# Attention over packed keys and two expert layers on one core: how W' is stored, which engine issues the word loads, and the order of the packed attention's steps

## The chip, the cores and the metric

The kernel runs on one core of one Trainium2 chip. The metric is device microseconds of one execution. The times given are medians of several runs; the profile is of one execution, and its span runs from the first to the last instruction.

## The reference

Inputs are q, k, v of 8 batches x 8 heads x 576 tokens x 64 and p of 8 x 8 x 32 x 64, all float32, and four float64 weight matrices. With 4608 tokens of width 512:

```
def sm_attn(qq, kk, vv):
    s = scale * np.matmul(qq, kk.transpose(0, 1, 3, 2))
    a = np.exp(s - np.max(s, axis=-1, keepdims=True))
    a = a / (np.sum(a, axis=-1, keepdims=True) + 1e-09)
    return np.matmul(a, vv)
p_packed = sm_attn(p, k, v)
out = sm_attn(q, p_packed, p_packed)
x = (tokens x 512 view of out)
h = x @ w_in;  g = h * np.cos(h);  x2 = g @ w_out          (first layer, w_in 512 x 2048)
h = x2 @ w_in2;  P = a0 + a1 h + a2 h^2 + a3 h^3
Q = 1 + |b0| |h| + |b1| h^2;  out = (P / (Q + 1e-6)) @ w_out2   (second layer)
```

## The kernel before, in words

Three stages follow each other, with some overlap.

The **packed attention** works on 16 groups (a batch and four of its heads). For group n the helper `prep` transposes k into kT on DVE (L180), `s1` makes the scores of p against k on PE (L189), their maximum (mx, L203) and scaled negative (nb, L205) on DVE, and the exponentials E on ScalarE (L208); `et` transposes E on PE (L224) and copies it to eT on ScalarE (L226); `pv` multiplies it with v on PE (L235), scales and masks the result into ppm on DVE (L239) and stores it to ppd; `ppt` transposes ppm on PE (L258) and splits it into the high and low part wl (L66 ScalarE, L67 DVE). pbd is p transposed into blocks, at the start, on DVE (L168). The second attention of batch 0 is woven in between (`attn2_steps`).

The **W' stage** multiplies wl with w_in, so that h later comes straight from the attention weights. There are 16 units (4 column blocks fq x 4 head pairs hp), and in each unit 4 tiles (P, a pair of batches) of 128x512 on PE (L275). A tile is evicted from the accumulator by ScalarE (L286), the third of each unit by DVE (L284), into one of four wev buffers, and stored to the scratch tensors wd. `load_wq` brings the parts of wd that a batch needs back as wq, and `split_wq` divides them into high and low part. Four of the first layer's slots (below) run early, in between.

The weights are float64 and are read as pairs of 32-bit words. A load brings 128x1024 words (512 KB) into one of three st64 buffers; `convert` makes a float32 pair from them: ScalarE scales the low word (L80), DVE does three integer steps on the high word (L82, L87, L90), GpSimd multiplies (L91, the last reader of st64), DVE adds (L92), ScalarE rounds to the high part (L93), GpSimd subtracts for the low part (L94). `conv_next` emits one conversion and the load three conversions ahead.

The **rest** is PE's: 128 slots of the first layer (h L520, y L567) and then the second layer (L671, L729).

The program is written in one order, and a scheduler then decides for each engine in which order its instructions stand; an engine's queue runs strictly in that order. The DMA queues are SP's (k, v, q, words, wq) and ScalarE's (ppd, W' stores).

Of the kernel before, what the change touches and what calls it, by code (L numbers as in the profile page):

```python
# [20 lines left out]
def pack_attention_moe_moe_kernel(  # L21
# [78 lines left out]
    NP = B // 2  # L100
    wd = [dram.tile([B, G, 128, 512], F32, name=f"wd{i}") for i in range(NQ)]
    ppd = [dram.tile([128, 4 * D], F32, name=f"ppd{n}") for n in range(NG)]
# [10 lines left out]
    if True:  # L113
# [19 lines left out]
        def load_v(n):  # L133
            b, g = divmod(n, G)
            t = wv.tile([96, 4, 6 * D], F32, tag="vx", bufs=3, name="vx")
            nc.sync.dma_start(out=t, in_=v[b, 4 * g:4 * g + 4].rearrange("h (x r) d -> x h (r d)", r=6))
            vx_t[n] = t
# [22 lines left out]
        for h in range(4):  # L160
            nc.gpsimd.memset(mask[32 * h:32 * h + 32, h, :], 1.0)
        load_kv(1)

        pbd = wv.tile([128, NG, NDB, 4, M], F32, name="pbd")
# [10 lines left out]
        def prep(n):  # L175
            b, g = divmod(n, G)
            kT = wk.tile([128, NDB, 6, 32, 3], F32, tag="kT", bufs=2, name="kT")
            kx = kx_t.pop(n)
            for e in range(NDB):
                nc.vector.transpose(  # L180
                    out=kT[:, e].rearrange("p r j a -> p a r j"),
                    in_=kx[:, :, 32 * e:32 * e + 32].rearrange("p (a r) i -> p a r i", a=3),
                )
            kT_t[n] = kT.rearrange("p e r j a -> p e (r j a)")

# [79 lines left out]
        def wunit(x):  # L265
            fq, hp = cv1[x]
            wi = w1i_t.pop(x)
            g, gg = divmod(hp, 2)
            dst = wd[fq].rearrange("(c b) g p f -> c b g p f", b=2)
            for P in range(NP):  # L270
                t = we_p.tile([128, 512], F32, tag="wev", bufs=4, name="wev")
                ps = psw.tile([128, 512], F32, tag="w", bufs=2, name="w")
                wl = wl_t[P]
                for i, (a, c) in enumerate(PASSES):
                    nc.tensor.matmul(  # L275
                        out=ps,
                        lhsT=wl[a][:, hp].rearrange("p b m -> p (b m)"),
                        rhs=wi[c],
                        start=(i == 0),
                        stop=(i == 2),  # L280
                    )

                if P == 2:
                    nc.vector.tensor_scalar(out=t, in0=ps, scalar1=INV2PI, scalar2=None, op0=ALU.mult)  # L284
                else:
                    nc.scalar.activation(out=t, in_=ps, func=AF.Copy, scale=INV2PI)  # L286
                for b2 in range(2):
                    nc.scalar.dma_start(out=dst[P, b2, g, 64 * gg:64 * gg + 64], in_=t[64 * b2:64 * b2 + 64])  # L288

# [62 lines left out]

        def load_st(x, src):
            t = cv_p.tile([128, 512, 2], U32, tag="st64", bufs=3, name="st64")
            if len(src.shape) == 4:
                ld = nc.sync.dma_start(out=t.rearrange("p (k f) t -> p k f t", k=NKD), in_=src)
            else:
                ld = nc.sync.dma_start(out=t, in_=src)
            st_t[x] = t
            return ld  # L360
# [5 lines left out]
        def load_w1i(x):  # L366
            fq, hp = cv1[x]
            load_st(("i", x), words(w1i[128 * hp:128 * hp + 128, 512 * fq:512 * fq + 512]))

# [6 lines left out]
        def load_w1o(f):  # L376
            load_st(f, words(w1o[128 * f:128 * f + 128, :]))

# [27 lines left out]
        for i in range(3):  # L406
# [4 lines left out]
            0, wk, lambda nm: ps0.tile([128, 2, 512], F32, tag="s1", bufs=2, name=nm), tg0, lambda: None  # L411
        )
        for n in range(NG + 1):
            if n >= 3:
                next(at, 1)
            if n < NG:
                s1(n)
                if n + 2 < NG:
                    load_kv(n + 2)
            if n >= 1:  # L420
                pv(n - 1)
            if n + 1 < NG:
                prep(n + 1)
            if n < NG:
                et(n)
            if n % 3 and at_cv[0] < NA:
                conv_next()
            if n >= 1:
                ppt(n - 1)
# [12 lines left out]
        def load_wq(b, j):  # L442
            t = wo_p.tile([128, G, 2, 512], F32R, tag="wq", bufs=5, name="wq")
            nc.sync.dma_start(
                out=t[:, :, 1, :].bitcast(F32),
                in_=wd[j][b].rearrange("g p f -> p g f"),
            )
            wq_t[b, j] = t
# [5 lines left out]
        def load_w2(i):  # L454
# [3 lines left out]
            else:  # L458
                src = words(w2o[128 * f:128 * f + 128, :])
            hold(load_st(("w2", i), src), last_h[0])  # L460

# [167 lines left out]
        for x in range(len(cv1)):  # L629
# [4 lines left out]
            if x in more:  # L634
                conv_next()
            if hp == NKD - 1:
                load_wq(0, fq)
            if fq > 0 and hp == 2:
                split_wq(0, fq - 1, nc.vector)
            if x in early:  # L640
                slot(early.index(x))
        e0.close()
        at_p = e1t.enter_context(tc.tile_pool(name="at", bufs=1, side="right", **RW))
# [147 lines left out]
```

## Time and profile before

| | us |
|---|---|
| median of 3 runs (lowest, highest) | 1713.13 (1712.69, 1714.67) |
| the profiled execution's own time | 1714.48 |
| its span | 1712.7 |
| PE busy | 1616.1 (94%) |
| DVE busy | 1325.6 (77%) |
| ScalarE (ACT) busy | 1197.7 (70%) |
| GpSimd (POOL) busy | 184.8 (11%) |
| mean granted TensorE clock | 0.981 of full speed |

A share of the span is an average over stages with different limits, and PE's matmuls are pipelined with modelled ends. Issuing a DMA is not counted as busy: a queue can be full while its engine looks idle. "ACTq" and "SPq" are the queues of ScalarE and SP.

### The profile page before, as it was taken

What the parts mean: (1) busy time and instruction counts of PE and PEld (TensorE: products, weight loads), DVE (VectorE), ACT (ScalarE), POOL (GpSimd) and SP (SyncE); (2) the same over time, 40 slices, a digit from 0 to 9 for tenths busy, and PEclk for the clock granted to TensorE, in tenths of its full rate; (3) what the DMA queues carried; (4) which work ended last, traced back from release to release, by engine and by line L of the source; (5) the groups of instructions that cost most, each with busy time, mean ns of one, the idle gap of its engine ahead of it and who ended that gap; (6) DMA issues with size and microseconds to landing.
All of it is one profiled execution on the core that took longest, in us unless ns stands there. A gap on an engine that the chain in (4) does not pass through costs nothing.

```text
span 1712.7 us, 23880 instructions
## 1 busy us (share of the span) xinstructions
PE 1616.1 (94%) x8832; PEld 1408.8 (82%) x8832; DVE 1325.6 (77%) x2054; ACT 1197.7 (70%) x1933; POOL 184.8 (11%) x140
## 2 busy tenths in 40 slices
PE   6786768999999999999999999999999999999996
PEld 4674658999999999999998888888888888888884
DVE  8954665879787888878548888888888888888884
ACT  3434645767676777767659787778777878787874
POOL 4303540012121211121000000000000000000000
PEclk9998888999999999999999999999999999999998
DMA  9857773434343443434276101101020202020100
GB/s 303 264 162 197 225 206 102 133 125 154 131 156 120 143 153 122 144 131 151 90 259 214 50 25 37 38 24 51 1 74 1 74 1 74 1 74 1 41 10 25
DMA packets 104372, 183.49 MB, mean 107 GB/s; under 512 B 12096, under 2 KB 46912, under 8 KB 104256
## 3 DMA queue, kind: packets, MB, share of 16 engines
q1 hardware_dynamic: 91712, 163.09, 29.4%
q10 hardware_dynamic: 12544, 18.88, 4.2%
q8 instruction: 69, 1.13, 0.3%
q14 instruction: 47, 0.39, 0.1%
HBM read 117.97 MB, written 63.96 MB: 106 GB/s over the span
## 4 chain that ended last, share of the span: by engine, by line
PE 79%; DVE 4%; ACT 3%; issue 1%; DMA 1%; ACTq 1%; POOL 1%; DVEq 0%; POOLq 0%; SPq 0%
PE h L671 23%; PE o L729 23%; PE y L567 20%; PE h L520 11%; PE s L189 2%; ACTq L288 1%; DVE g L552 1%; ACT u L545 1%; PE w L275 0%; POOL cvp L91 0%; DVE cvf L87 0%; ACT r L550 0%; ACT r L551 0%; DVE sT L340 0%; DVE cvf L82 0%
## 5 line engine op out<-in xcount | busy, mean ns | idle before, releaser
L567 PE MATMUL y<-gh,w1o 128*128 128x288 f32 x2048 | 432.7, 297 | 0.4
L671 PE MATMUL h<-x,w 128*128 128x512 f32 x1728 | 422.2, 393 | 0.0
L671 PEld LDWEIGHTS h<-x,w 128*128 128x128 f32 x1728 | 324.1, 188 | 74.3
L567 PEld LDWEIGHTS y<-gh,w1o 128*128 128x128 f32 x2048 | 337.0, 189 | 2.7 <-DVE yl L67 1.1
L729 PE MATMUL o<-w,g2h 128*128 128x512 f32 x1152 | 332.9, 393 | 1.3 <-ACT g2h L689 1.3
L567 PE MATMUL y<-gl,w1o 128*128 128x288 f32 x1024 | 296.2, 295 | 1.0 <-DVE gl L67 1.0
L729 PEld LDWEIGHTS o<-w,g2h 128*128 128x128 f32 x1152 | 216.1, 188 | 51.1 <-ACT g2h L689 2.1
L520 PE MATMUL h<-ah,wq 128*128 128x288 f32 x1024 | 234.0, 305 | 19.5 <-DVE g L552 14.2
L729 PE MATMUL o<-w,g2l 128*128 128x512 f32 x576 | 199.9, 393 | 0.0
L520 PEld LDWEIGHTS h<-ah,wq 128*128 128x128 f32 x1024 | 177.4, 195 | 26.4 <-issue 17.7
L704 ACT ACTIVATE sq<-h 128x512 f32<-128x512 f32 x144 | 87.4, 607 | 156.1 <-PE h L671 156.1
L567 PEld LDWEIGHTS y<-gl,w1o 128*128 128x128 f32 x1024 | 193.4, 189 | 2.5 <-DVE gl L67 1.9
L706 DVE SCALAR_TENSOR_TENSOR ab<-sq,coef,ab 128x512 f32<-128x512 f32 x144 | 108.1, 751 | 66.7 <-ACT ab L705 66.6
L545 ACT ACTIVATE u<-h,coef 128x576 f32<-128x576 f32 x128 | 94.2, 737 | 87.7 <-PE h L520 87.1
L520 PE MATMUL h<-al,wq 128*128 128x288 f32 x512 | 154.8, 302 | 0.0
L552 DVE SCALAR_TENSOR_TENSOR g<-h,r 128x576 f32<-128x576 f32 x128 | 96.0, 753 | 62.7 <-ACT r L551 62.4
L91 POOL TENSOR_TENSOR cvp<-st,cvp 128x512 f32<-128x512 f32 x64 | 89.8, 1403 | 469.2 <-DVE cvp L90 192.2
L715 DVE SCALAR_TENSOR_TENSOR ab<-ab,y 128x512 f32<-128x512 f32 x144 | 99.5, 691 | 48.2 <-ACT y L712 48.2
L729 PEld LDWEIGHTS o<-w,g2l 128*128 128x128 f32 x576 | 108.1, 188 | 24.6
L546 DVE SCALAR_TENSOR_TENSOR r<-u,h 128x576 f32<-128x576 f32 x128 | 95.4, 747 | 36.4 <-ACT u L545 35.6
L707 ACT ACTIVATE c<-h,coef 128x512 f32<-128x512 f32 x144 | 114.1, 792 | 8.3 <-DVE g2l L695 8.3
L67 DVE TENSOR_TENSOR gl<-g,gh 128x576 fp32r<-128x576 f32 x128 | 102.8, 804 | 21.4 <-ACT gh L66 19.8
(88 smaller groups left out, 2498.8 us busy)
## 6 DMA issues: line engine op xcount, KB each, us to landing
x<-yd SPq DMA_DIRECT2D x36, 512.0 KB
w<-w2d SPq DMA_DIRECT2D x68, 256.0 KB
st<-in_moe_w_out_dram SPq DMA_DIRECT2D x32, 512.0 KB
st<-in_moe_w_in_dram SPq DMA_DIRECT2D x32, 512.0 KB
wd<-wev ACTq DMA_DIRECT2D x128, 128.0 KB
wq<-wd SPq DMA_DIRECT2D x32, 512.0 KB
kx<-in_k_dram SPq DMA_DIRECT2D x16, 576.0 KB
vx<-in_v_dram SPq DMA_DIRECT2D x16, 576.0 KB
```

The source lines that it names most:

```text
L67: lo_eng.tensor_tensor(out=lo, in0=src, in1=hi.bitcast(F32), op=ALU.subtract)
L91: nc.gpsimd.tensor_tensor(out=pf, in0=dl, in1=pf, op=ALU.mult)
L520: last_h[0] = nc.tensor.matmul(out=ps[:, u, 0:HS], lhsT=wq[:, g, a, o:o + 128], rhs=a_t[b, g][c][:, hf * HS:hf * HS + HS], start=(i == 0), ...
L545: nc.scalar.activation(out=u, in_=ph, func=AF.Identity, bias=coef[:, 6:7])
L546: nc.vector.scalar_tensor_tensor(out=r, in0=u, scalar=RND, in1=ph, op0=ALU.subtract, op1=ALU.subtract)
L552: nc.vector.scalar_tensor_tensor(out=gt, in0=ph, scalar=2.0 * math.pi, in1=r, op0=ALU.mult, op1=ALU.mult)
L567: nc.tensor.matmul(out=y_t[d][:, 0:HS], lhsT=w1o_s[f // 4][a][:, f % 4, 128 * d:128 * d + 128], rhs=gs[c][:, u], start=(f == 0 and i == 0) ...
L671: nc.tensor.matmul(out=ps, lhsT=w2_s[f][:, 0, a, 128 * kk:128 * kk + 128], rhs=x_t[t, c, kk], start=(i == 0), stop=(i == 3 * NKD - 1),)
L706: nc.vector.scalar_tensor_tensor(out=ab, in0=sq, scalar=coef[:, 5:6], in1=ab, op0=ALU.mult, op1=ALU.add)
L707: nc.scalar.activation(out=c1, in_=ph, func=AF.Identity, scale=coef[:, 3:4], bias=coef[:, 2:3])
L715: nc.vector.scalar_tensor_tensor(out=ab, in0=ab, scalar=QC, in1=y0, op0=ALU.add, op1=ALU.mult)
L729: nc.tensor.matmul(out=o_t[s], lhsT=g2_t[n][a][:, 128 * s:128 * s + 128], rhs=w2_s[f][:, 1, c], start=(f == 0 and i == 0), stop=(f == NFC ...
```

## The change

Four things are changed.

- wd is laid out so that one evicted 128x512 tile is one contiguous block, and each tile is stored in one transfer by SP instead of two halves by ScalarE. `load_wq` then reads its part as two transfers of 64 partitions, and the loads for batch 0 are written one unit later.
- The loads of words of the first layer's weights go to ScalarE's queue; those of the second layer stay on SP's.
- In the packed attention the scores of group n+1 are written ahead of E's transposes of group n, and these ahead of the v product of group n-1; k is transposed two groups ahead and loaded three ahead.
- kT and E have their columns in another order, so that kT is written in runs of 32 elements (before, every third element). v's rows follow: each v load becomes three loads of 32 partitions.

```
-    wd = [dram.tile([B, G, 128, 512], F32, name=f"wd{i}") for i in range(NQ)]
+    wd = [dram.tile([NP, NKD, 128, 512], F32, name=f"wd{i}") for i in range(NQ)]
...
-            nc.sync.dma_start(out=t, in_=v[b, 4 * g:4 * g + 4].rearrange("h (x r) d -> x h (r d)", r=6))
+            for a in range(3):
+                nc.sync.dma_start(
+                    out=t[32 * a:32 * a + 32],
+                    in_=v[b, 4 * g:4 * g + 4].rearrange("h (j a r) d -> a j h (r d)", a=3, r=6)[a],
+                )
...
         load_kv(1)
+        load_k(2)
...
-            kT = wk.tile([128, NDB, 6, 32, 3], F32, tag="kT", bufs=2, name="kT")
+            kT = wk.tile([128, NDB, 6, 3, 32], F32, tag="kT", bufs=2, name="kT")
...
-                    out=kT[:, e].rearrange("p r j a -> p a r j"),
+                    out=kT[:, e].rearrange("p r a j -> p a r j"),
...
-                for b2 in range(2):
-                    nc.scalar.dma_start(out=dst[P, b2, g, 64 * gg:64 * gg + 64], in_=t[64 * b2:64 * b2 + 64])
+                nc.sync.dma_start(out=wd[fq][P, hp], in_=t)
...
-        def load_st(x, src):
+        def load_st(x, src, eng):
...
-            load_st(("i", x), words(w1i[128 * hp:128 * hp + 128, 512 * fq:512 * fq + 512]))
+            load_st(("i", x), words(w1i[128 * hp:128 * hp + 128, 512 * fq:512 * fq + 512]), nc.scalar)
...
-            load_st(f, words(w1o[128 * f:128 * f + 128, :]))
+            load_st(f, words(w1o[128 * f:128 * f + 128, :]), nc.scalar)
...
+        s1(0)
+        prep(1)
         for n in range(NG + 1):
             if n >= 3:
                 next(at, 1)
+            if n + 1 < NG:
+                s1(n + 1)
+            if n + 3 < NG:
+                load_k(n + 3)
+            if n + 2 < NG:
+                load_v(n + 2)
+                prep(n + 2)
             if n < NG:
-                s1(n)
-                if n + 2 < NG:
-                    load_kv(n + 2)
+                et(n)
             if n >= 1:
                 pv(n - 1)
-            if n + 1 < NG:
-                prep(n + 1)
-            if n < NG:
-                et(n)
...
-            nc.sync.dma_start(
-                out=t[:, :, 1, :].bitcast(F32),
-                in_=wd[j][b].rearrange("g p f -> p g f"),
-            )
+            P, b2 = divmod(b, 2)
+            src = wd[j][P].rearrange("(g c) (b p) f -> c b p g f", c=2, b=2)
+            for gg in range(2):
+                nc.sync.dma_start(out=t[64 * gg:64 * gg + 64, :, 1, :].bitcast(F32), in_=src[gg, b2])
...
-            if hp == NKD - 1:
-                load_wq(0, fq)
+            if fq > 0 and hp == 0:
+                load_wq(0, fq - 1)
...
+        load_wq(0, NQ - 1)
```

How the order of instructions moves, at three places. First, ScalarE's queue at the start of the W' stage; wev is an evicted tile, wd_60 the first column block's scratch, st the words, w1i and w1o converted weights. Before:

```order
L286 ACTIVATE wev<-w 128x512 x2
L288 DMA wd_60<-wev 64x512 x6
L286 ACTIVATE wev<-w 128x512
L93 ACTIVATE w1i_1125<-cvf 128x512
L286 ACTIVATE wev<-w 128x512
L288 DMA wd_60<-wev 64x512 x4
L286 ACTIVATE wev<-w 128x512
L288 DMA wd_60<-wev 64x512 x4
```

And with the change, a little later, where the first load of words stands behind nine evictions:

```order
L289 ACTIVATE wev<-w 128x512 x3
L360 DMA st_1261<-in_moe_w_in_dram 128x1024
L289 ACTIVATE wev<-w 128x512
L93 ACTIVATE w1i_1249<-cvf 128x512
L289 ACTIVATE wev<-w 128x512
L360 DMA st_1275<-in_moe_w_out_dram 128x1024
L80 ACTIVATE st_1261<-st_1261 128x512
L93 ACTIVATE w1o<-cvf 128x512
L289 ACTIVATE wev<-w 128x512 x3
L360 DMA st_1317<-in_moe_w_in_dram 128x1024
L80 ACTIVATE st_1275<-st_1275 128x512
```

The 128 stores are gone from this queue, and 16 loads stand between the evictions, each some rows ahead of the L80 that reads it.

Second, SP's queue at the same place. Before, and then with the change:

```order
L136 DMA vx<-in_v_dram 96x4x384 x2
L358 DMA st_1241<-in_moe_w_in_dram 128x1024
L358 DMA st_1255<-in_moe_w_out_dram 128x1024
L444 DMA wq<-wd_60 128x2x512
L358 DMA st_1301<-in_moe_w_in_dram 128x1024
```

```order
L137 DMA vx<-in_v_dram 32x4x384 x15
L290 DMA wd_60<-wev 128x512 x11
L452 DMA wq<-wd_60 64x2x512
L290 DMA wd_60<-wev 128x512 x5
L452 DMA wq<-wd_60 64x2x512
L290 DMA wd_61<-wev 128x512 x12
```

Where loads of words stood, the stores stand now, one a tile, with the two halves of each wq load in between.

Third, the first groups of the packed attention. PE before, and then with the change:

```order
L189 MATMUL s_155<-kT,pbd 128x288 x4
L189 MATMUL s_186<-kT,pbd 128x288 x4
L224 MATMUL et<-ident,E 96x128 x6
L235 MATMUL pv<-vx,eT 128x256 x6
L224 MATMUL et<-ident,E 96x128 x6
L189 MATMUL s_248<-kT,pbd 128x288 x4
L258 MATMUL pt<-ident,ppm 128x128 x2
L235 MATMUL pv<-vx,eT 128x256 x6
```

```order
L194 MATMUL s_161<-kT,pbd 128x288 x4
L194 MATMUL s_179<-kT,pbd 128x288 x4
L229 MATMUL et<-ident,E 96x128 x6
L194 MATMUL s_212<-kT,pbd 128x288 x4
L240 MATMUL pv<-vx,eT 128x256 x6
L229 MATMUL et<-ident,E 96x128 x6
L194 MATMUL s_276<-kT,pbd 128x288 x4
L263 MATMUL pt<-ident,ppm 128x128 x2
L229 MATMUL et<-ident,E 96x128 x6
L240 MATMUL pv<-vx,eT 128x256 x6
```

The third scores stand ahead of the first v product, and from the third group on E's transposes stand ahead of the v product of the group before.

DVE at the same place, with the change:

```order
L185 STREAM_TRANSPOSE kT<-kx 128x3x6x32 x2
L82 TENSOR_SCALAR cvf<-st_155 128x512
L87 SCALAR_TENSOR_TENSOR cvf<-st_155,cvf 128x512
L90 TENSOR_SCALAR cvp<-cvf 128x512
L173 STREAM_TRANSPOSE pbd<-px 32x4x32 x4
L173 STREAM_TRANSPOSE pbd<-px 32x28x32 x4
L92 TENSOR_TENSOR cvf<-cvf,cvp 128x512
L82 TENSOR_SCALAR cvf<-st_157 128x512
L152 TENSOR_SCALAR coef<-par 128x4
L153 TENSOR_SCALAR coef<-par 128x2
L208 TENSOR_REDUCE mx<-s_161 128x1
L87 SCALAR_TENSOR_TENSOR cvf<-st_157,cvf 128x512
```

The steps of the first conversion and part of the second stand ahead of the first maximum; before, the transposes of p and k alone stood ahead of it.

## Rows read from the trace of the kernel before

**Rows 1.** By stage: length; busy PE, PEld, DVE, ACT, POOL; granted clock, DMA share, GB/s.

```profile
0.00:133.25 133.25, 102.89 (x464) 79.62 (x464) 103.09 (x213) 48.57 (x95) 38.28 (x36) 0.96 0.79 236
133.25:266.00 132.75, 92.08 (x360) 67.41 (x360) 79.58 (x112) 67.34 (x113) 55.71 (x40) 0.86 0.78 216
266.00:1712.70 1446.70, 1421.15 (x8008) 1261.76 (x8008) 1142.96 (x1730) 1081.79 (x1726) 90.84 (x64) 0.99 0.26 85
```

**Rows 2.** Timeline of ScalarE near the W' stage's end: start, length, work, [idle before, releaser].

```profile
251.25 1.09 ACT L286 ACTIVATE wev<-w 128x512 f32<-128x512 f32 x2 [2.04 <-PE w L275]
251.88 2.39 ACTq L288 DMA_DIRECT2D wd<-wev  x4
```

**Rows 3.** The line of the W' stores: shortest, median and longest ns, first and last start.

```profile
L288 ACTq DMA_DIRECT2D wd<-wev x128: 452/607/849, 135.0 to 259.9; - x128
```

**Rows 4.** Chain of waits, 133 to 266 us: shares by line, and its longest transfers.

```profile
by line: issue 11.6%; ACTq L288 9.9%; PE h L520 9.2%; PE w L275 6.2%; POOL cvp L91 5.7%; DMA wd<-wev 5.0%; ACT wev L286 4.0%; DVE cvf L82 3.9%; DMA st<-in_moe_w_out_dram 3.7%; DVE cvf L87 3.6%; DMA st<-in_moe_w_in_dram 3.3%; DVE cvp L90 3.2
...
144.81 4.41 DMA st<-in_moe_w_in_dram
186.12 4.33 DMA wd<-wev
190.51 4.19 DMA wq<-wd
203.92 4.94 DMA st<-in_moe_w_out_dram
```

**Rows 5.** Waits of ScalarE, 133.25 to 266 us: total, times, longest.

```profile
ACT wev L286 <- PE w L275: 20.2, 13, 2.5
```

**Rows 6.** Issues by SP, by line: a 128x512 store, word loads.

```profile
L466 SPq DMA_DIRECT2D w2d<-cvh x32: 319/320/877, 339.9 to 817.0; - x32
...
L358 SPq DMA_DIRECT2D st<-in_moe_w_in_dram x16: 328/328/346, 40.7 to 216.9; - x16
```

**Rows 7.** Waits of SP's queue, 133 to 266 us.

```profile
SPq L358 <- POOL cvp L91: 37.7, 15, 5.0
```

**Rows 8.** Transfers of 133 to 266 us, and the table by stage for 0 to 60.

```profile
DMA packets 14328, 28.71 MB, mean 216 GB/s; under 512 B 2432, under 2 KB 2673, under 8 KB 14321
...
0.00:60.00 60.00, 43.28 (x189) 32.05 (x190) 53.96 (x105) 22.61 (x43) 23.69 (x26) 1.00 0.97 302
```

**Rows 9.** Waits of PE from 18.89 to 133.25 us.

```profile
PE pt L258 <- DVE ppm L239: 7.1, 4, 3.9
PE pv L235 <- ACT eT L226: 5.6, 6, 1.5
PE et L224 <- ACT E L208: 3.6, 1, 3.6
PE s L189 <- DVE kT L180: 1.3, 2, 1.1
```

**Rows 10.** Groups by line of DVE, 0 to 135 us: count, busy us, mean ns, idle before.

```profile
L180 DVE STREAM_TRANSPOSE kT<-kx 128x576 f32<-128x576 f32 x32 | 28.1, 937 | 5.5 <-DMA kx<-in_k_dram 5.5
L87 DVE SCALAR_TENSOR_TENSOR cvf<-st,cvf 128x512 uint32<-128x512 uint32 x13 | 10.7, 825 | 0.1
L92 DVE TENSOR_TENSOR cvf<-cvf,cvp 128x512 f32<-128x512 f32 x13 | 9.3, 718 | 0.2 <-POOL cvp L91 0.2
...
L311 DVE STREAM_TRANSPOSE qT<-qx 128x1152 f32<-128x1152 f32 x2 | 2.7, 1335 | 0.0
```

**Rows 11.** Timeline of DVE and PE: first transpose of p, first scores.

```profile
6.91 0.30 DVE L168 STREAM_TRANSPOSE pbd<-px 32x128 f32<-32x128 f32 x1 [0.55 <-DMA px<-in_p_dram]
8.84 4.10 PE L189 MATMUL s<-kT,pbd 128*128 128x288 f32 x8 [8.84 <-DVE pbd L168]
```

**Rows 12.** Two v products in PE's timeline, and the first one's stretch by stage columns.

```profile
85.36 5.33 PE L235 MATMUL pv<-vx,eT 96*128 96x256 f32 x12
...
93.67 2.76 PE L235 MATMUL pv<-vx,eT 96*128 96x256 f32 x12
...
85.36:90.48 5.12, 5.12 (x13) 3.92 (x13) 3.73 (x10) 0.83 (x2) 0.42 (x1) 0.50 1.00 277
```

More of the change, by code (lines that the diff above doesn't have):

```diff
@@ L180, in prep @@
                 nc.vector.transpose(
-                    out=kT[:, e].rearrange("p r j a -> p a r j"),
+                    out=kT[:, e].rearrange("p r a j -> p a r j"),
                     in_=kx[:, :, 32 * e:32 * e + 32].rearrange("p (a r) i -> p a r i", a=3),
                 )
-            kT_t[n] = kT.rearrange("p e r j a -> p e (r j a)")
+            kT_t[n] = kT.rearrange("p e r a j -> p e (r a j)")
         def scores(ps, lhs, rhs):
@@ L267, in wunit @@
             wi = w1i_t.pop(x)
-            g, gg = divmod(hp, 2)
-            dst = wd[fq].rearrange("(c b) g p f -> c b g p f", b=2)
             for P in range(NP):
@@ L351, in pack_attention_moe_moe_kernel @@
         st_t = {}
-        def load_st(x, src):
+        def load_st(x, src, eng):
             t = cv_p.tile([128, 512, 2], U32, tag="st64", bufs=3, name="st64")
             if len(src.shape) == 4:
-                ld = nc.sync.dma_start(out=t.rearrange("p (k f) t -> p k f t", k=NKD), in_=src)
+                ld = eng.dma_start(out=t.rearrange("p (k f) t -> p k f t", k=NKD), in_=src)
             else:
-                ld = nc.sync.dma_start(out=t, in_=src)
+                ld = eng.dma_start(out=t, in_=src)
             st_t[x] = t
@@ L459, in load_w2 @@
                 src = words(w2o[128 * f:128 * f + 128, :])
-            hold(load_st(("w2", i), src), last_h[0])
+            hold(load_st(("w2", i), src, nc.sync), last_h[0])
         def conv_w2(i):
```

## The prediction, made before the result

> **What bounds the kernel now.** I read the table by stage first, since only one total is in the page and the stages have different limits [rows 1]. I cut it into three: the packed attention up to 133.25 us (the first product of W'), the W' stage up to 266 us, and the rest, where PE is busy 1421.15 of 1446.7 us. The last stage is PE's own work and the change leaves its products alone, so what the change is worth comes from the first 266 us, and each microsecond by which the last stage starts earlier counts in full. Now the timeline of ScalarE near the end of the W' stage [rows 2]: two evictions, then four stores issued in 2.4 us, and so on; an eviction nominally waits for PE, but PE itself has two accumulators and waits for the evictions behind the same queue. Then the stores' line [rows 3]: 128 issues of 607 ns are 77.7 us of ScalarE's queue in a stage of 132.75 us in which ScalarE computes 67.34 us [rows 1]. Together that is more than the stage (an issue may overlap the activation before it), so ScalarE's queue bounds the W' stage. The chain of waits in the stage agrees [rows 4]: the store issues are its longest entry with a line, 9.9% of 133 us = 13.2 us. In the first stage no engine is full; PE is busy 102.89 of 133.25 us, and I read who kept it waiting after its first v product at 18.89 us [rows 9]: E's transposes, the copies of E transposed, and the scaled product, which comes from DVE, busy 54 of the first 60 us [rows 8].
>
> **The W' stage, step by step.** Removed from ScalarE: 128 issues, 77.7 us. Added to it: 16 loads of words (the order of the changed program has 16 behind the first eviction). None is issued from ScalarE today; the same loads take 0.33 us on SP [rows 6], so 16 x 0.33 = 5.3 us. The loads also bring two waits. First, landing: a load lands 4.41 to 4.94 us after its issue [rows 4], and ScalarE's own first step of the conversion (L80) stands a few rows behind the load in the same queue. For the first one, two evictions (0.6), one rounding (0.6) and one issue (0.3) stand between, 2.1 us, so it stalls some 2.6 us; done so for all 16 at 4.7 us, six or seven are short by 1 to 3 us and the rest by nothing or little, 13 us in sum. Second, buffers: a load waits until GpSimd has read the old words; SP waits 37.7 us for that in 15 waits today [rows 7], 2.5 us each, which costs nothing there. On ScalarE it would hold the evictions behind it. I take it as nothing, because the scheduler has put each load some 4 us of ScalarE's rows behind the L80 that feeds the GpSimd step; the price if that cover is gone is the third rival. ScalarE's other waits stay: 20.2 us for PE's W' products [rows 5]. Sum: 67.3 + 5.3 + 13 + 20.2 = 105.8, **106 us for 132.75: a gain of 27**. From below, the transfers: 28.71 MB move in this stage [rows 8], at the 302 GB/s of the first 60 us, when the DMA engines were 97% busy, they need 95 us (gain 38). From above, only the issue time that lies on the chain comes back, 13.2 us (119.6 us). I take the middle because it is built from the queue that bounds the stage.
>
> What goes to SP is hidden. A store of the same 128x512 shape takes SP 0.32 us to issue [rows 6], 64 of them 20 us in 106. Each wq load becomes two; 32 more issues, at the 0.33 us of the other loads [rows 6], are 10.5 us of SP over the whole run, each far ahead of its use. Loading wq one unit later (a unit is then 106/16 = 6.6 us) still leaves over a unit for the 4.19 us that it takes to land [rows 4] before its split. The four eviction buffers give a store 4 x 1.66 = 6.6 us to come back, against 0.6 + 0.3 + 4.33 us for eviction, issue and the slowest landing [rows 4]. That cover is thin; if it goes, see the fourth rival.
>
> The Trainium skill ("DMA: Bandwidth & Descriptors", section "Issuing engines are not separate DMA queues") speaks against this part: transfers from all queues run on the same 16 DMA engines, so another queue saves only the issue time, "which is usually small relative to the DMA itself". Here the row shows issue time that is not small, 77.7 us [rows 3]. By the rule's "usually small" the gain would be that of the second rival, 13.2 us.
>
> **The packed attention, step by step.** Between 18.89 and 133.25 us PE waits 7.1 us for the scaled product, 5.6 for the copy of E transposed, 3.6 for E and 1.3 for k transposed, 17.6 in all [rows 9]. Scores a group earlier put E's chain under other products, so I take its 3.6 and the 1.3 of k as gone. With E's transposes ahead of the v product, the copy runs under that product's 2.76 us [rows 12]: 5.6 gone. The 7.1 us belong to DVE, which gets lighter: kT is now written in runs of 32 instead of every third element. No trace shows that, the nearest row is the transpose of q, written in runs, 1335 ns for 1152 columns against 937 for 576 [rows 10]; at half of 1335, 32 transposes save 32 x 0.27 = 8.6 us of DVE (nothing, if the stride is not the reason). I take half of the 7.1 as gone, 3.5. Together 3.6 + 1.3 + 5.6 + 3.5 = 14.0.
>
> Against this stands a later start. The first three loads of words, 1.57 MB, are now issued at once from ScalarE beside k and p, while today they follow p on SP's queue. At 302 GB/s they need 5.2 us; half of that in front of p, 2.6 us, delays the transposes of p that start at 6.91 and the first scores at 8.84 [rows 11]. In DVE's new order the steps L92 and L87 of the first conversions, 0.72 + 0.83 us [rows 10], also stand ahead of the first nb, which waits for the first scores (the other steps of the first conversion run while p is on its way). So the first v product comes 4.2 us later. The v loads in thirds cost SP 32 more issues, 10.5 us in 133, hidden. Net **14.0 - 4.2 = 9.8, say 10 us**. Bounds: all 17.6 go, +13; none goes, -4. PE's clock helps a little and is not counted: right after PE's longest wait for the scaled product, 3.9 us [rows 9], a v product took 5.33 us instead of 2.76, at a granted clock of 0.50, the lower level of 1.2 GHz [rows 12].
>
> **Sum.** 27 + 10 = 37 us. The profiled execution took 1714.48 us, 1.8 more than its span, and gives 1677.5; the median of the runs shown is 1.35 us under it, so 1676.
>
> **Rivals.** (1) Larger: the W' stage falls to its transfers and every wait of PE in the first stage goes: 38 + 13 = 51 us, **1662**. For it: DVE 79.58, PE 92.08 and GpSimd 55.71 us of work in the stage [rows 1] all fit into 95. Against it: PE's granted clock there is 0.86 of 2.4 GHz and conversions have a long chain across four engines.
> (2) Smaller: the stores leave the chain, but conversions take their place (load, ScalarE, DVE, GpSimd, DVE, ScalarE), and the first stage only breaks even. Then 13.2 us come back, **1700**. For it: GpSimd, the loads of words and DVE's conversion steps already make up 23% of the chain [rows 4].
> (3) Slower: ScalarE stands behind the loads. It has 132.75 - 67.3 - 5.3 = 60 us to lose before the stage is longer than today; with 16 loads that is 3.8 us a load, the point from which this decides. If each load waits 2.5 us for GpSimd [rows 7] and its landing is not covered for another 4.7 us [rows 4], the stage takes 72.6 + 16 x 7.2 = 188 us at most; halfway between that and the point, 5.5 us a load, it takes 160.6, 28 us more: **1741**. Against it: the new order has other work between.
> (4) No gain: SP is held by wq loads that wait for stores to land, eight halves x 4.33 us = 35 us, and the stores behind them starve the four eviction buffers; with the 27 us of the W' stage spent on that and the first stage even, the time stays at **1713**.
>
> **How the numbers follow.** Forecast 0.60; rival 1 0.15, rival 2 0.16, rival 3 0.05, rival 4 0.04. Faster by over 0.2% (3.4 us, about what a measurement of this kernel tells from no change) in the first three: 0.91; same 0.04; slower 0.05. The range runs from a little under rival 1 to a little over rival 2, 1658 to 1702, and leaves out rivals 3 and 4 and about as much again for cases that I have not thought of.
>
> **What would show it.** Right: the first W' product near 123 us and the last stage from near 229 us; the table by stage with ScalarE's W' stage near 106 us; no store issues on ScalarE; kT transposes near 670 to 750 ns; PE's wait for E and for its transposed copy gone. Wrong: long waits of ScalarE's queue for GpSimd or for the landing of words (rival 3), waits of evictions for stores (rival 4), a first stage no shorter because PE starts late or DVE holds it. A W' stage of 95 us at 300 GB/s is rival 1; a chain of conversions is rival 2.

## The result, and the profile after

The changed kernel takes 1693.69 us (median; 1691.34 to 1694.30) against 1713.90 for the kernel before beside it: 20.2 us less, a ratio of 0.9879 with a 95% interval of 0.9862 to 0.9896. The forecast was 1676 us, a gain of 37; the direction and the range held, the size was missed by about half, and the time lies nearer to rival 2's 1700 than to the forecast. The profiled execution took 1694.3 us with a span of 1692.5.

The table by stage of the changed kernel, cut at its first W' product and as far from the end as before (columns as in [rows 1]):

```profile
0.00:134.56 134.56, 99.37 (x464) 78.73 (x464) 98.52 (x213) 47.87 (x95) 36.91 (x36) 0.96 0.83 233
134.56:245.80 111.24, 86.12 (x363) 61.40 (x364) 88.42 (x112) 69.32 (x113) 56.78 (x40) 0.88 0.79 257
245.80:1692.50 1446.70, 1420.58 (x8006) 1260.93 (x8005) 1142.02 (x1730) 1081.10 (x1725) 90.43 (x64) 0.99 0.27 85
```

Against [rows 1], the last stage holds the same work in the same time (8006 products for 8008). The whole gain is the W' stage, 132.75 to 111.24 us, 21.5 less (forecast 27). The packed attention, from which 10 us were to come, is 1.3 us longer.

**The packed attention.** First, the chain of waits at the start, and then the timelines of DVE and PE:

```profile
1.20 11.30 DMA px<-in_p_dram
```

```profile
12.60 5.73 DVE L173 STREAM_TRANSPOSE pbd<-px 32x128 f32<-32x128 f32 x8 [2.88 <-DMA px<-in_p_dram]
```

```profile
13.99 4.18 PE L194 MATMUL s<-kT,pbd 128*128 128x288 f32 x8 [13.99 <-DVE pbd L173]
22.42 3.77 PE L194 MATMUL s<-kT,pbd 128*128 128x288 f32 x8 [4.25 <-DVE kT L185]
26.03 0.82 PE L229 MATMUL et<-ident,E 128*96 128x128 f32 x6
26.68 2.11 PE L194 MATMUL s<-kT,pbd 128*128 128x288 f32 x8
30.23 2.86 PE L240 MATMUL pv<-vx,eT 96*128 96x256 f32 x12 [1.44 <-ACT eT L231]
```

p takes 11.3 us to land, its transposes start at 12.60 instead of 6.91 and the first scores at 13.99 instead of 8.84 [rows 11]. The first v product comes at 30.23 instead of 18.89 [rows 9], 11.3 us later. ScalarE's timeline tells where the rest of these 11.3 us arises. Before, at the first exponential and the first copy of its transpose:

```profile
16.19 0.74 ACT L208 ACTIVATE E<-s,nb 128x576 f32<-128x576 f32 x1
...
18.03 0.81 ACT L226 ACTIVATE eT<-et 96x768 f32<-96x768 f32 x1 [0.43 <-PE et L224]
```

And of the changed kernel, the same two steps, and a later place where a load of words stands:

```profile
23.15 0.74 ACT L213 ACTIVATE E<-s,nb 128x576 f32<-128x576 f32 x1 [3.43 <-DVE nb L210]
...
24.91 0.33 ACTq L360 DMA_DIRECT2D st<-in_moe_w_out_dram  x1
27.84 0.63 ACT L93 ACTIVATE w1o<-cvf 128x512 fp32r<-128x512 f32 x1 [3.85 <-DVE cvf L92]
28.37 0.65 ACT L80 ACTIVATE st<-st 128x512 f32<-128x512 uint32 x1
28.99 0.34 ACTq L360 DMA_DIRECT2D st<-in_moe_w_out_dram  x1
29.37 0.81 ACT L231 ACTIVATE eT<-et 96x768 f32<-96x768 f32 x1 [0.35 <-POOL cvp L91]
...
86.92 0.34 ACTq L360 DMA_DIRECT2D st<-in_moe_w_in_dram  x1
91.91 0.67 ACT L80 ACTIVATE st<-st 128x512 f32<-128x512 uint32 x1 [4.85 <-DMA st<-in_moe_w_in_dram]
...
92.48 0.79 ACT L231 ACTIVATE eT<-et 96x768 f32<-96x768 f32 x1
93.17 0.73 ACT L213 ACTIVATE E<-s,nb 128x576 f32<-128x576 f32 x1
```

The exponential starts 23.15 - 16.19 = 7.0 us later: 5.15 from the scores and 1.8 from DVE (1.55 were forecast). The maximum itself comes 0.7 us sooner behind the scores than before, but between it and its negative DVE now has a conversion step (L87, 1.49 us) and the second group's transposes of k (1.42 us). From the exponential to the copy it took 1.8 us before and takes 6.2 now, 4.4 more. Part of that is PE: the second group's scores stand ahead of E's transposes, as before, but start at 22.42, because they wait for DVE's second transpose of k; so E's transposes, for which E was there at 24, end at 26.85. The other 2.5 us are ScalarE's queue: the copy of E transposed could run at 26.85, but stands behind a rounding that waits for DVE, an L80, and a load of words released by GpSimd; it runs at 29.37. At 87 us the same queue stands 4.85 us for the landing of words, with a copy and an exponential behind it.

From the first v product to the first W' product it is now 104.3 us instead of 114.4. That is 10.0 us less, but not 10 us of waits. The stretch by stage columns, before and after:

```profile
18.89:133.25 114.36, 95.48 (x442) 75.14 (x442) 89.86 (x187) 44.40 (x89) 32.98 (x24) 0.96 0.76 229
```

```profile
30.23:134.56 104.33, 88.82 (x434) 71.65 (x434) 78.60 (x177) 41.23 (x85) 25.12 (x19) 0.97 0.79 220
```

PE's idle time in it fell from 18.9 to 15.5 us, so the waits gave 3.4 us of the 14 forecast. The other 6.7 us are PE's own work: eight products (the third scores) now run ahead of the first v product, and the same 192 v products took 44.2 us instead of 47.3. Who kept PE waiting in that stretch:

```profile
PE et L229 <- ACT E L213: 9.7, 4, 5.3
PE s L194 <- ACT E L213: 2.8, 1, 2.8
PE pt L263 <- DVE ppm L244: 1.9, 3, 0.8
PE pv L240 <- ACT eT L231: 1.4, 1, 1.4
```

Against [rows 9] the scaled product fell from 7.1 to 1.9 us and the copy of E transposed from 5.6 to 1.4, but E itself rose from 3.6 to 12.5 (the first two lines together).

**The W' stage.** By line, the stores on SP, the loads of words on ScalarE and the halved wq loads on SP (shortest, median and longest ns, first and last start):

```profile
L290 SPq DMA_DIRECT2D wd<-wev x64: 319/320/877, 136.2 to 236.8; - x64
...
L360 ACTq DMA_DIRECT2D st<-in_moe_w_in_dram x16: 334/334/390, 41.7 to 209.4; - x16
...
L452 SPq DMA_DIRECT2D wq<-wd x64: 573/580/708, 146.5 to 783.3; - x64
```

What ScalarE waited for in this stage:

```profile
ACT wev L289 <- PE w L278: 10.1, 10, 1.4
ACT w1o L93 <- DVE cvf L92: 7.2, 5, 3.7
ACT w1i L93 <- DVE cvf L92: 3.9, 4, 2.1
ACT wev L289 <- DMA wd<-wev: 3.8, 3, 1.7
...
ACT st L80 <- DMA st<-in_moe_w_in_dram: 2.5, 3, 1.0
...
ACT st L80 <- DMA st<-in_moe_w_out_dram: 1.2, 2, 0.8
```

Waits for PE halved (20.2 in [rows 5]), and the landing of words costs 3.7 us. Roundings wait 11.1 us for DVE, which is busy 88.42 of 111.24 us; before it was 2.5. Evictions wait 3.8 us for a store to free their buffer. That is not new. Before, by the same view (there the idle time ahead of an eviction also holds the issuing of stores):

```profile
ACT wev L286 <- DMA wd<-wev: 9.2, 4, 3.2
```

At the end PE stands still, in PE's timeline and in the chain of waits:

```profile
244.26 0.61 PE L525 MATMUL h<-ah,wq 128*128 128x288 f32 x1 [5.62 <-ACT wq L66]
```

```profile
237.19 5.94 DMA wq<-wd
```

The second half of the last wq load is issued at 237.19 us, after the last stores, lands 5.94 us later and is then split; PE waits 5.62 us for it. Not all of that is new: the kernel before, too, has a wait of PE at this place, for a step of the first layer on DVE:

```profile
266.04 0.58 PE L520 MATMUL h<-ah,wq 128*128 128x288 f32 x1 [4.55 <-DVE g L552]
```

### The profile page after: what moved, and what is told of

Its sections match the earlier page's. It is cut to its first block, busy times and chain, and to the rows that moved or that the text cites. A ratio compares the mean times of both kernels' runs of the same rounds, so it can differ in the third digit from the quotient of the medians.

```text
span 1692.5 us, 23934 instructions
## 1 busy us (share of the span) xinstructions
PE 1606.1 (95%) x8832; PEld 1401.1 (83%) x8832; DVE 1329.0 (79%) x2054; ACT 1198.3 (71%) x1933; POOL 184.1 (11%) x140
## 4 chain that ended last, share of the span: by engine, by line
PE 82%; DVE 7%; DMA 4%; ACT 4%; issue 2%; POOL 0%; SPq 0%; ACTq 0%; POOLq 0%; DVEq 0%
PE h L677 24%; PE o L735 23%; PE y L572 20%; PE h L525 10%; PE s L194 2%; PE pv L240 2%; DVE cvf L87 1%; DMA st<-in_moe_w_in_dram 1%; PE w L278 1%; DMA st<-in_moe_w_out_dram 1%; DVE g L557 1%; DMA px<-in_p_dram 1%; DMA wq<-wd 1%; DVE cvf L82 1%; DMA wd<-wev 1%
## 5 line engine op out<-in xcount | busy, mean ns | idle before, releaser
L525 PE MATMUL h<-ah,wq 128*128 128x288 f32 x1024 | 228.9, 300 | 17.8 <-DVE g L557 7.4
L525 PEld LDWEIGHTS h<-ah,wq 128*128 128x128 f32 x1024 | 173.4, 191 | 23.9 <-issue 11.4
L735 PEld LDWEIGHTS o<-w,g2l 128*128 128x128 f32 x576 | 108.2, 188 | 24.7
L713 ACT ACTIVATE c<-h,coef 128x512 f32<-128x512 f32 x144 | 114.0, 792 | 8.4 <-DVE g2l L701 8.4
```

The costliest lines, as they stand in the source:

```text
L525: last_h[0] = nc.tensor.matmul(out=ps[:, u, 0:HS], lhsT=wq[:, g, a, o:o + 128], rhs=a_t[b, g][c][:, hf * HS:hf * HS + HS], start=(i == 0), ...
L713: nc.scalar.activation(out=c1, in_=ph, func=AF.Identity, scale=coef[:, 3:4], bias=coef[:, 2:3])
L735: nc.tensor.matmul(out=o_t[s], lhsT=g2_t[n][a][:, 128 * s:128 * s + 128], rhs=w2_s[f][:, 1, c], start=(f == 0 and i == 0), stop=(f == NFC ...
```

## The experiments

Twelve runs were made, in three groups, each group on one chip beside the kernel before. The length of the W' stage is the span less 1446.7 us (the last stage, taken as unchanged) less the start of the first W' product.

| kernel | median us (range) | ratio [95%] | first scores | first v product | first W' product | W' stage |
|---|---|---|---|---|---|---|
| before | 1713.90 | 1 | 8.84 | 18.89 | 133.25 | 132.75 |
| the change | 1693.69 | 0.9879 [0.9862, 0.9896] | 13.99 | 30.23 | 134.56 | 111.2 |
| words3 | 1686.97 (1685.76 to 1688.09) | 0.9845 [0.9816, 0.9874] | 9.04 | 21.86 | 128.86 | 110.4 |
| words16 | 1685.24 (1684.14 to 1685.74) | 0.9834 [0.9805, 0.9862] | 9.07 | 23.51 | 125.33 | 111.9 |
| words99 | 1688.96 (1684.43 to 1693.49) | 0.9856 [0.9822, 0.9891] | 9.02 | 25.71 | 129.42 | 110.5 |
| store_sp | 1695.40 (1692.72 to 1697.80) | 0.9889 [0.9852, 0.9926] | | | 136.50 | 112.8 |
| store_act | 1699.26 (1697.74 to 1701.70) | 0.9919 [0.9900, 0.9937] | | | 130.17 | 119.1 |
| halves_sp | 1699.80 (1698.86 to 1700.98) | 0.9923 [0.9903, 0.9943] | | | 132.75 | 117.5 |
| w16_oldkT | 1688.24 (1682.81 to 1689.69) | 0.9847 [0.9823, 0.9871] | | | 127.89 | 113.1 |
| w16_oldorder | 1694.63 (1689.80 to 1699.20) | 0.9890 [0.9858, 0.9922] | | 20.00 | 138.31 | 112.2 |
| words_act | 1721.43 (1718.61 to 1726.96) | 1.0035 [1.0019, 1.0050] | 13.22 | 29.95 | 138.18 | 135.0 |
| words16_again | 1691.97 (1691.80 to 1694.61) | 0.9853 [0.9833, 0.9874] | 8.88 | 26.05 | 133.49 | 110.1 |
| w16_late | 1693.26 (1689.02 to 1697.02) | 0.9863 [0.9830, 0.9895] | 8.87 | 26.38 | 127.45 | 114.0 |
| w16_three | 1694.09 (1692.93 to 1697.39) | 0.9865 [0.9843, 0.9887] | 8.92 | 25.62 | 133.79 | 112.9 |

The kernel before ran at a median of 1711.27 us beside words3, words16, words99 and store_sp, at 1713.57 beside the next four, and at 1715.18 beside the last four. words16_again came out 4 us above the range expected for it, w16_late and w16_three 9 and 10 us; the other times lie in the ranges of one of their theories or within 1 us of them. First scores, v product, W' product and W' stage are of one profiled execution each.

**Which queue loads the words.** In words3, words16 and words99 the first 3, the first 16 and all loads of the first layer's words are issued by SP again; the rest of the change stays.

```
+        loads = [0]
+
+        def words_eng():
+            loads[0] += 1
+            return nc.sync if loads[0] <= 3 else nc.scalar
...
-            load_st(f, words(w1o[128 * f:128 * f + 128, :]), nc.scalar)
+            load_st(f, words(w1o[128 * f:128 * f + 128, :]), words_eng())
```

> The change with the first three loads of words back on SP's queue; the other 29 stay on ScalarE's. Theory A (the first stage gained nothing because the word loads on ScalarE's queue get in its way: the first three delay p by 5.7 us and the first v product by 11.3 us): p lands near 7 us again, the first scores start near 9 to 10 us instead of 13.99, the first v product near 21 instead of 30.23, and the run is 5 to 9 us faster than the change, 1685 to 1689 us. Rival B (the new order itself gains nothing, since the stage is held by its transfers): the late start is made up elsewhere, within 2 us of the change, 1692 to 1696 us.

> The change with the first 16 loads of words (all of the packed attention) on SP's queue, the 16 of the W' stage on ScalarE's. Theory A, its second half (ScalarE's conversion step L80 stands in its queue ahead of the exponentials and waits for words that were issued late, so PE waits 9.7 us for E): the first stage ends near 122 to 125 us instead of 134.56, the run takes 1682 to 1685 us. Rival B: the stage still ends at 130 us or later, and SP's loads of k and v wait behind those of words; 1690 us or more.

> The change with all loads of words on SP's queue, as before the change. Theory C (in the W' stage only taking the stores off ScalarE counts): within 3 us of the run with 16 on SP, 1682 to 1688 us. Rival D (the word loads had to leave SP, since stores that wait for evictions would hold them there): the W' stage is 6 us or more longer than the 111 us of the change, with SP's word loads waiting behind stores and ScalarE's L80 waiting for words.

The opposite, words_act, is the kernel before with nothing but these loads moved:

```
-                ld = nc.sync.dma_start(out=t, in_=src)
+                ld = eng.dma_start(out=t, in_=src)
...
-            load_st(f, words(w1o[128 * f:128 * f + 128, :]))
+            load_st(f, words(w1o[128 * f:128 * f + 128, :]), nc.scalar)
```

> The kernel before with one part of the change alone: the first layer's words are loaded by ScalarE, the stores stay two halves a tile by ScalarE as well. Theory A (the first three loads, issued from a second queue at once, delay p): the first scores start near 14 us instead of 8.84, the first v product 6 to 11 us later than 18.89, and the W' stage gets 16 issues of 0.33 us more on ScalarE, which bounds it, so it takes 133 to 140 us: 1719 to 1727 us, slower. Rival (the late start of the change came from its new order on DVE, not from the queue): first scores within 1 us of 8.84, and the time within 6 us of before.

The first scores in PE's timeline, of words16 and then of words_act:

```profile
9.07 3.96 PE L194 MATMUL s<-kT,pbd 128*128 128x288 f32 x8 [9.07 <-DVE pbd L173]
```

```profile
13.22 4.17 PE L189 MATMUL s<-kT,pbd 128*128 128x288 f32 x8 [13.22 <-DVE pbd L168]
```

Three loads back on SP bring the first scores back by 5 us, and moving the words in the kernel before takes them away by 4.4, so the late first scores are the queue's. The first v product needs more care: at 29.95 us in words_act it is as late as with the whole change, but words_act has the old order only as written. As executed, its third scores stand ahead of the first v product, and its conversion steps ahead of the first maximum, as in the change; the scheduler moved them when the loads moved. With the new order and the first loads on SP (words3, words16, words99) those conversion steps stand behind the maximum again, and the first v product comes at 21.9 to 25.7 us. So the move of the first loads brought 4.5 to 8.4 of the 11.3 us, in part through the order that came with it; the rest stays with the new order.

Moving the words alone makes the kernel before slower by 6.0 us (0.35%, 3.3 to 8.6 by its interval); in the profiled executions 4.9 us of it lie in the first stage and 2.3 in the W' stage. That a load on ScalarE's queue also costs behind the start is likely but not shown: PE's wait for E in the first stage is 7.7 us in words3 and 4.8 in words16, yet their medians differ by 1.7 us, less than the first stage of one kernel scatters (words16 and words16_again, 125.33 and 133.49). In the W' stage it makes no difference who loads the words: 110.4, 111.9 and 110.5 us, although in words99 ScalarE waits 13.7 us for landings, against 3.7 in the change:

```profile
ACT st L80 <- DMA st<-in_moe_w_in_dram: 8.9, 6, 2.8
ACT st L80 <- DMA st<-in_moe_w_out_dram: 4.8, 4, 1.9
```

So the stores on SP do not need the words to leave it, which the change had arranged.

**The stores alone.** store_sp is the kernel before with the first part of the change only: the new layout of wd, one transfer a tile by SP, wq in two halves a unit later.

```
-                for b2 in range(2):
-                    nc.scalar.dma_start(out=dst[P, b2, g, 64 * gg:64 * gg + 64], in_=t[64 * b2:64 * b2 + 64])
+                nc.sync.dma_start(out=wd[fq][P, hp], in_=t)
```

> The kernel before with the store part alone: the new layout of wd, one transfer a tile issued by SP, the halved wq loads one unit later. Words stay on SP, the order of the first stage stays. Theory C (the stores are the whole gain of the W' stage): the first stage ends near 133 us, the W' stage takes 109 to 114 us, the run 1690 to 1695 us, a gain of 19 to 23 us. Rival D: word loads and stores collide on SP, the W' stage takes 118 us or more, the run 1699 us or more.

The W' stage is 112.8 us: 19.9 of the 21.5 us gained there belong to this part. By its ratio it gains 0.0111 x 1714 = 19 us of the whole (12.7 to 25.4 by the interval).

It does two things at once, one transfer for two and SP for ScalarE, and they were taken apart. In store_act ScalarE issues the one transfer (`nc.scalar` for `nc.sync` in the diff above; wq comes in halves as in store_sp). In halves_sp SP issues the old two halves into the old layout, and wq is loaded whole, a unit later:

```
-                    nc.scalar.dma_start(out=dst[P, b2, g, 64 * gg:64 * gg + 64], in_=t[64 * b2:64 * b2 + 64])
+                    nc.sync.dma_start(out=dst[P, b2, g, 64 * gg:64 * gg + 64], in_=t[64 * b2:64 * b2 + 64])
```

> The kernel before with one transfer a tile, but still issued by ScalarE: 64 issues instead of 128. Theory E (the long issue belongs to the shape: 64 partitions take 0.58 to 0.61 us on SP and on ScalarE, 128 take 0.32 to 0.38): an issue takes 0.33 us, 64 of them 21 us instead of 77.7, and the W' stage comes close to that of the run with the stores on SP, 113 to 118 us, a run of 1694 to 1701 us. Rival F (ScalarE has to be rid of the stores): 0.5 us or more an issue, each still ahead of the next eviction, a W' stage of 120 us or more, 1702 us or more.

> The kernel before with the two half stores a tile issued by SP, in the old layout, wq loads in one transfer. Theory E: each half takes 0.6 us to issue on SP too, 128 of them 77 us of SP in the stage, still free of ScalarE: a W' stage of 112 to 118 us, 1693 to 1700 us. Rival F: 0.33 us an issue on SP, so the time was ScalarE's own; same as the run with whole tiles on SP.

The stores' lines of store_act and of halves_sp:

```profile
L285 ACTq DMA_DIRECT2D wd<-wev x64: 326/327/694, 131.9 to 239.0; - x64
```

```profile
L288 SPq DMA_DIRECT2D wd<-wev x128: 445/554/1322, 134.4 to 245.7; - x128
```

A 128x512 tile takes 0.327 us to issue on ScalarE and 0.320 on SP; a half of it, 64x512, takes 0.607 on ScalarE [rows 3] and 0.554 on SP. The long issue goes with the half transfers (and the old layout, which goes with them) on either engine, so merging alone takes 128 x 0.607 - 64 x 0.327 = 57 us off ScalarE's queue. That brings the stage to 119.1 us (-13.6). Moving alone takes off all 77.7 and brings it to 117.5 (-15.3); both together give 110 to 114. Each gets most of the gain; the two do not add, as is to be expected once a queue no longer bounds.

All three runs also load wq a unit later, and no run has that alone. Little of the gain can come from it: in the kernel before SP's wq loads do wait 38.2 us for stores in this stage, with the words behind them, but ScalarE waits only 2.7 us there for words, and PE 2.0 us for wq.

**Order and layout of the packed attention.** Both start from words16. w16_oldkT has the old layout of kT and E with one v load; w16_oldorder has the old order of the steps with the new layout. w16_oldkT does not change the layout alone: the scheduler put its third scores behind the first v product again.

```
-            kT = wk.tile([128, NDB, 6, 3, 32], F32, tag="kT", bufs=2, name="kT")
+            kT = wk.tile([128, NDB, 6, 32, 3], F32, tag="kT", bufs=2, name="kT")
```

> The version with 16 loads of words on SP, with the old layout of kT and E and the v load in one transfer; the new order stays. Theory G (the layout is worth something because DVE holds PE): kT transposes take 935 ns again instead of 720, 7 us more of DVE, and half of it or more shows: 3 to 7 us slower than the version with the new layout, 1688 to 1692 us. Rival H (DVE's time is covered, and thirds of the v load cost as much): within 2 us of it, 1683 to 1687.

```
-            if n + 1 < NG:
-                s1(n + 1)
...
             if n < NG:
-                et(n)
+                s1(n)
...
+            if n < NG:
+                et(n)
```

> The version with 16 loads of words on SP, with the old order of the packed attention; the new layout stays. Theory I (the order is what shortens the first stage): PE's waits for the scaled product and for E's copy come back, the first stage ends near 131 to 134 us instead of 125.3, 1690 to 1694 us. Rival J (the lighter DVE did it): within 2 us, 1683 to 1687.

The transposes of k by line, in words16 and in w16_oldkT, and then PE's waits from 26 to 139 us in w16_oldorder:

```profile
L185 DVE STREAM_TRANSPOSE kT<-kx 128x576 f32<-128x576 f32 x32 | 22.8, 749 | 6.7 <-DMA kx<-in_k_dram 6.7
```

```profile
L181 DVE STREAM_TRANSPOSE kT<-kx 128x576 f32<-128x576 f32 x32 | 28.2, 937 | 6.6 <-DMA kx<-in_k_dram 6.6
```

```profile
PE pt L262 <- DVE ppm L243: 10.1, 5, 4.7
PE et L228 <- ACT E L212: 5.3, 1, 5.3
PE pv L239 <- ACT eT L230: 4.3, 5, 1.1
```

The layout saves 937 - 749 = 188 ns a transpose, 6 us of DVE, and 3 us of the median, within the scatter: its worth is not settled. The order is worth about 9.6 us by the ratios of w16_oldorder and words16, 6.3 by that of words16_again, with an interval of some 7 us on either, so by the second it could be nothing. The waits for the scaled product, E and its copy are at 19.7 us, against 9.0 in words16, though the first v product, at 20.00, comes 3.5 us earlier. The new order starts later and stalls less.

PE's idle time in the first stage (its length less PE's busy time) tells the kernels apart better than the length, since the busy time for the same products scatters from 99.4 to 106.3 us. It is 28.6 to 33.0 us in the five traces with the old order and the words on SP (before, store_sp, store_act, halves_sp, w16_oldorder), and 24.7 to 28.3 in the seven with the new order and the first three loads or more on SP. In the change it is 35.2, in words_act 34.0. So the order as written saves some 4 us of idle time, and the words on ScalarE's queue cost about as much in the old order and 9 in the new.

**The wait at the end of the W' stage.** In w16_late and w16_three, both from words16, the early slots of the first layer are moved, so that more of PE's work should stand where it waits for the last wq. words16_again runs beside them.

```
-        early = (6, 8, 11, 13)
+        early = (7, 10, 13, 15)
```

> words16 with the four early slots of the first layer each placed one or two units later (after units 7, 10, 13 and 15 instead of 6, 8, 11 and 13). Theory F (the W' stage ends with PE waiting 5 us for wq because the last tiles have to be stored, loaded back and split, and PE has no other work left): with a slot's work after the last unit the wait shrinks by 2 to 4 us, and the time is 1681 to 1684 us. Rival (the slots then run in the way of the last evictions on ScalarE, and the last store comes later by as much): 1685 to 1688 us.

```
-        early = (6, 8, 11, 13)
+        early = (7, 9, 12)
```

> words16 with three early slots (after units 7, 9 and 12) instead of four, so that one slot more (24 first-layer products into h and 24 into y, about 4 us of PE) stands behind the last W' unit and ahead of the products that need the last wq. Theory F: the 5 us wait of PE for wq shrinks to 1 or 2 us and the last stage takes no longer for it: 1681 to 1684 us. Rival (the W' stage does not get shorter by the slot that left it, and the slot's work is added behind): 1686 to 1690 us.

> words16 once more, beside its two variants on the same chip: 1684 to 1688 us, and a second execution's view of the wait for wq at the end of the W' stage, 4 to 6 us.

The groups by line of PE from 130 us to the end of the wait, in words16_again and in w16_three (operands, shape, count, busy us, mean ns):

```profile
L577 PE MATMUL y<-gh,w1o 128*128 128x288 f32 x64 | 15.5, 325 | 0.0
L530 PE MATMUL h<-ah,wq 128*128 128x288 f32 x48 | 12.9, 343 | 4.2 <-DVE g L562 1.3 <-DVE wq L67 1.2 <-ACT wev L289 1.0
```

```profile
L577 PE MATMUL y<-gh,w1o 128*128 128x288 f32 x64 | 13.8, 300 | 1.3 <-ACT gh L66 1.3
L530 PE MATMUL h<-ah,wq 128*128 128x288 f32 x48 | 12.4, 333 | 4.6 <-ACT wev L289 2.1 <-DVE g L562 1.3 <-ACT wq L66 1.1
```

The wait stays at 5.58 and 5.49 us (5.57 in words16_again), and the times do not fall. The edits did not do what they were meant to: in all three the same 64 and 48 products stand between the start of the stage and the wait; the scheduler placed the slots so. So these two runs do not judge the theory; how to fill the wait stays open.

words16 beats both kernels by its medians (1685.24 and, on another chip, 1691.97). Against the change its ratios of 0.9834 and 0.9853 stand for 4 to 8 us, but the second interval, to 0.9874, still overlaps that of the change, from 0.9862.

## Why the prediction was right, and where its sizes were off

**That ScalarE's queue bounded the W' stage** held. With the stores merged alone the stage lost 13.6 us, with the same bytes issued by the same engine; with the same half stores issued by SP it lost 15.3. The rule of the Trainium skill that was weighed ("DMA: Bandwidth & Descriptors", section "Issuing engines are not separate DMA queues") allows a gain from the issue time only and calls it usually small. Halves_sp does not contradict its first half: those 15.3 us are less than the 77.7 us of issue taken off. Nor is one issue, 0.607 us [rows 3], large beside the slowest landing, 4.33 us [rows 4]. What decided here is the number of issues: 128 of them, 77.7 us, in one engine's queue and a stage of 132.75.

**The size of that gain**, 27 forecast, is 21.5. The sum "67.3 + 5.3 + 13 + 20.2" came near, 105.8 for 111.24, by terms that miss in both directions: ScalarE computes 69.3 us and stands idle, issues included, for 41.9 instead of 38.5. The landing stalls, 13, measured 3.7. The waits for PE, 20.2, measured 10.1: "ScalarE's other waits stay" failed, since PE had waited for the evictions. Put at nothing were 11.1 us of roundings behind DVE and 3.8 us behind the eviction buffers (the "thin cover", without becoming rival 4). At the end of the stage PE waits 5.62 us for the last wq; the step that failed there is "loading wq one unit later still leaves over a unit": that is so for three of the four column blocks, but behind the last one no unit is left. The sum treated the stage as one queue's; once that queue was relieved the stage became a chain across engines. Rival 2 named this turn, but priced it too high, with 13.2 us back in all.

**The first stage**, from which 10 us were to come, came out 1.3 us longer, as rival 2 had it ("the first stage only breaks even"). That the time still fell inside the range it owes to the W' stage, and to a range drawn past rival 2. Two steps failed.

**The late start** was the largest miss: 4.2 forecast, 11.3 measured, of which 8.2 are idle time of PE and 3.1 work that now stands ahead of the first v product. The 2.6 us for p assumed that half of the three loads' 5.2 us goes ahead of it; 5.15 us came, as much as if all of it had. DVE's 1.55 were 1.8. Not counted were 4.4 us between the first exponential and its copy: the second scores, late for want of k transposed, ahead of E's transposes on PE, and a load and conversion steps ahead of the copy on ScalarE. Here was the mechanism of rival 3, the queue standing behind a load, in the stage for which I had not asked.

**The waits to go**, 14.0, gave 3.4 us of PE's idle time behind the first v product; the stretch is 10.0 us shorter mainly because PE had 6.7 us less work in it, which the forecast did not count. The copy of E transposed went nearly as forecast (5.6 to 1.4). The scaled product did better (7.1 to 1.9), but not by the lighter DVE alone: with it and the old order PE waits 10.1 us (w16_oldorder), though a transpose of k takes 748 ns, at the edge of 670 to 750. "I take its 3.6 as gone" failed: E's wait rose to 12.5 us, with exponentials standing behind a landing of words on ScalarE (the 4.85 us at 87 us) and behind DVE's queue. With the first loads back on SP it is 4.8 to 7.7 (words16, words16_again, words99, words3), still more than the 3.6 that were to go. So the words' queue explains a part of the rise, and the new order did not hide E's chain either.

By the parts, if they add: the stores -19 us (store_sp), the words +6 (words_act), which leaves -20.7 + 19 - 6 = -7.7 for order and layout, in line with the 6.3 to 9.6 of w16_oldorder, and uncertain by as much. One of the change's parts, the words on ScalarE's queue, took back part of what another gained, and nothing in the W' stage needed it.

## What to carry to other kernels

Issue time belongs into the sum of an engine's queue: read it by shape, and see whether a transfer of the whole tile issues faster than its halves. Before a load moves to a second queue, look what is urgent on the first: a transfer issued at the same time from another queue still delays it (here by 5 us), and every step of the issuing engine then stands behind the load's wait and its landing. Where a scheduler sets the order, compare the executed order of every variant: an edit of a queue or a layout moved other steps here too. Once the bounding queue is relieved, cost the stage again as a chain, its last piece above all, where nothing is left to hide a store, a load and a split.

## What the runs showed of the hardware that was not expected

- **Issue time rises when a tile is cut.** 128x512 in one transfer takes 0.32 us on SP and 0.33 on ScalarE, half of it 0.55 to 0.61. The wq load of 128 partitions took 0.371 us before (median of line L444 in the kernel before), its halves 0.580 each; a v load of 96 partitions 0.329, its thirds 0.424. The forecast had priced the added loads at 0.33. No run tells partitions and layout apart.
- **Three loads of 512 KB on another queue delay a load on SP's by about the whole time that they need at 302 GB/s,** 5.2 us by estimate, 4.4 to 5.15 us measured at the first scores (words_act, the change).
- **The first stage scatters by 8 us between executions of one kernel on two chips.** By stage in words16 and in words16_again, its first 30 us and the whole:

```profile
0.00:30.00 30.00, 15.01 (x52) 10.77 (x53) 21.25 (x45) 8.18 (x15) 10.32 (x16) 0.94 0.97 289
...
0.00:125.33 125.33, 100.60 (x464) 80.06 (x464) 99.05 (x213) 47.72 (x95) 37.57 (x36) 0.96 0.90 251
```

```profile
0.00:30.00 30.00, 16.53 (x50) 11.53 (x50) 18.73 (x42) 7.44 (x14) 9.39 (x16) 1.00 0.96 259
...
0.00:133.49 133.49, 106.30 (x465) 82.90 (x465) 99.50 (x213) 47.95 (x95) 37.83 (x36) 0.95 0.86 235
```

The DMA engines are as busy in the first 30 us (0.97 and 0.96) and move 289 and 259 GB/s. Of the 8.2 us between the two, 5.7 are PE's busy time for the same work and 2.5 its idle time. Why is not shown; by the stage's length alone, what is gained there by order is uncertain by as much.
